# Ten K and V loads of a two-layer decode kernel, cut into two or three transfers by rows

## The chip, the cores and the metric

The kernel runs on one core of a Trainium2 chip. The metric is the device time of one execution in microseconds. Before the change its median is 303.34 us over 2 runs (302.91 and 303.77). A profile is one further execution, taken with the hardware profiler; its own span is named below.

## The reference

One token per batch entry goes through two layers with the same weights. Each layer is attention on a cache, then a gated feed-forward part, both with a residual connection:

```python
B, Sq, D = 4, 1, 512
Hq, Hkv, Sk, Dh = 32, 8, 4096, 128
...
q = (x @ wq) split into 32 heads
k = jnp.repeat(k_cache, rep, axis=1)      # rep = 4 query heads for each K/V head
v = jnp.repeat(v_cache, rep, axis=1)
p = _softmax(q k^T * Dh ** -0.5)
A = (p v, heads side by side) @ wo
...
B = (_sigmoid(x w_gate) * (x w_up)) @ w_down
...
x = x + _A_ref(_layernorm(x), ...)
x = x + _B_ref(_layernorm(x), ...)
x = x + _A_ref(_layernorm(x), ...)
x = x + _B_ref(_layernorm(x), ...)
```

K and V of one batch entry and one K/V head are 4096 x 128 in bf16, 1 MB each. There are 4 x 8 such heads, so 32 MB of K and 32 MB of V, each wanted in both layers.

## The kernel before

**Units.** One pass of attention for one layer, batch entry and K/V head is a unit. `ORDER` (L22) fixes the order of the 64 units, in `seq`; a unit is named by its place there, 0 to 63, so "K 44" is the K cache of unit 44. Units are worked two at a time (a pair): DVE turns each K in 32 x 32 blocks in place (`k_turn`, L1164), PE forms the scores (`scores`, L1180), DVE takes maxima, ACT exponentials (L1265), PE turns them (L1310), ACT or DVE copies them out (L1344, L1338), and PE multiplies them with V (`pv`, L1414). The steps of neighbouring pairs are interleaved, and small matmuls of the projections and the feed-forward part are set between them by tables written out at the head of the file.

**Slots.** A load of K or V takes one of 12 slots in SBUF, each 128 partitions of 8 KB; the four parts of the space of `wq` become four more slots late in the run. Row p of a load is 32 tokens of 128 numbers, so 8 KB that lie together in DRAM go to partition p. Some heads stay in their slots from layer 0 to layer 1 (`RET`, L15) and are not loaded a second time.

**Order of the loads.** The string table `LOADS` (L92) fixes the order of all loads, weights among them; it doesn't depend on what is free. `pump` (L522) is called after most steps: while the next load in the list has a free slot, it hands SyncE one DMA (L550). A slot is free in the list as soon as the code has written the last use of its contents; SyncE itself then waits on the chip until that use has been done (matmul L1414 for V, L1180 for K), and everything behind waits with it, since SyncE issues in order. All loads go through this one queue.

The part of the order that the change touches, units left out that stay in their slots: V 40, **K 44, K 45, V 41, K 46, K 47**, K 48, **V 44, V 45, K 49, V 46, V 47**, V 48, K 52, V 49, K 53, K 54, and so on to V 56, then K 62, K 63 and V 58 to V 63. The loads in bold are the ten that are changed. The last two V loads are issued in four quarters each (`v_parts`, L517), whose pieces are 2 KB.

**Semaphores.** Each slot has a semaphore that its DMAs raise by 16; what uses the slot waits for the value that it has after the slot's latest load. `_Sched` (L194) keeps, for each tile, its last writer and its readers, and derives the waits: `group` (L215) records several instructions of one engine, puts the waits ahead of the first of them and hands the last one's token to later users. `dma` (L244) is `group` with a single function.

```python
            S.dma(
                "sp",
                (lambda dst, src: lambda e: e.dma_start(dst, src))(dst, src),
                f"d{s}" if s < NSLOT else f"wq{s - NSLOT}",
                writes=slot_keys(s),
            )
```

Of the kernel before, what the change touches and what calls it, by code (L numbers as in the profile page):

```python
# [171 lines left out]
)  # L172


class _Token:
# [135 lines left out]
def bass_interleave_layers__gqa_block_cached__glu_gated_glu__decode_kernel(  # L311
# [17 lines left out]
    P = 128  # L329
# [13 lines left out]
    NSLOT = 12  # L343
# [8 lines left out]
    S = _Sched()  # L352
# [144 lines left out]
    def slot_keys(s):  # L497
        return [f"s{s}"] + ([f"wq{s - NSLOT}"] if s >= NSLOT else [])

    def take():  # L500
        return free.pop(0)

    def by_quarters(n):
        return n < NU - 2 and SHARE[n // 2] > 5
# [5 lines left out]
    def v_parts(s, n):  # L510
        _, b, u = seq[n]
        rows = A_v_cache[b, u].rearrange("(a p j) d -> a p (j d)", a=4, p=P)
        for a in range(4):
            dst = slot[s][:, a * JG * DH:(a + 1) * JG * DH]
            S.dma(
                "sp",
                (lambda dst, src: lambda e: e.dma_start(dst, src))(dst, rows[a]),  # L517
                f"wo{4 * (n % 2) + a}",
                writes=[f"v{n % 2}_{a}"] + (slot_keys(s) if a == 0 else []),
            )  # L520

    def pump():  # L522
        while loads:
            kind, n = loads[-1]
            if kind in wparts:
                loads.pop()
                dst, src = wparts[kind](n)
                S.dma("sp", (lambda dst, src: lambda e: e.dma_start(dst, src))(dst, src), f"wo{n}" if kind == "wo" else kind, writes=[f"{kind}{n}"])  # L528
                continue
            if not free:  # L530
                return
            loads.pop()
            s = take()
            _, b, u = seq[n]
            if kind == "k":
                where["kn", n] = s
                src = A_k_cache[b, u].rearrange("(p j) d -> p (j d)", p=P)
            else:
                where["v", b, u] = s
                if n >= NU - 2:  # L540
                    v_parts(s, n)
                    continue
                src = A_v_cache[b, u].rearrange("(p j) d -> p (j d)", p=P)
            dst = slot[s][:, :]
            if kind == "v" and by_quarters(n):
                dst = dst.rearrange("p (a m) -> p a m", a=4)
                src = A_v_cache[b, u].rearrange("(a p j) d -> p a (j d)", a=4, p=P)
            S.dma(
                "sp",
                (lambda dst, src: lambda e: e.dma_start(dst, src))(dst, src),  # L550
                f"d{s}" if s < NSLOT else f"wq{s - NSLOT}",
                writes=slot_keys(s),
            )

# [6 lines left out]
    for k in range(KD):  # L561
        if k == 1:
# [5 lines left out]
            writes=[f"wq{k}"],  # L568
        )
    pump()  # L570

    dve(lambda e: e.memset(ones_f, 1.0), writes=["ones_f"])
# [18 lines left out]
    fns = []  # L591
# [882 lines left out]
    def o_turn(g):  # L1474
        p = g % 2
        many = 2 - PV_WIDE[g]
        s = stage.pop()
        o_raw = slot[s].bitcast(dt.float32)[:, 0:2 * P * many]
        act(lambda e: e.activation(o_raw, O_ps[p][:, 0:2 * P * many], ACTF.Copy), reads=[f"O{p}"], writes=slot_keys(s))
        fns = []  # L1480
        for n in range(2 * many):
            r = n * REP
            fns.append(
                (lambda n, r: lambda e: e.matmul(
                    O_ps[p][:, 0:2 * OW].rearrange("p (t w) -> p t w", t=2)[:, :, 0:REP],
                    lhsT=o_raw[:, n * P:(n + 1) * P],
                    rhs=o_sel[:, :, r:r + REP],
                    start=(n == 0),
                    stop=(n == 2 * many - 1),
                ))(n, r)  # L1490
            )
        S.group("pe", fns, reads=slot_keys(s) + ["o_sel"], writes=[f"O{p}"])
        free.append(s)
        pump()
# [113 lines left out]
    for m in wo_steps.pop((-1, 0), ()):  # L1608
        wo_turn(m, (M_ps, S_ps)[m % 2], "MS"[m % 2])
    k_turn(0)  # L1610
    pump()
    k_turn(1)
    pump()
# [17 lines left out]
    for b in range(Bn):  # L1631
        n = vstep[last[0, b]] - 1
# [499 lines left out]
```

## Time and profile before

| what | value |
|---|---|
| median of 2 runs | 303.34 us |
| span of the profiled execution | 306.1 us |
| PE busy | 224.3 us, 73% |
| DVE busy | 205.7 us, 67% |
| ACT busy | 131.2 us, 43% |
| DMA packets of the kernel's own queue | 93.9% of 16 engines' span |
| bytes read from HBM | 116.66 MB, 381 GB/s over the span |

How to read it: the span runs from the first to the last instruction of the profiled execution; that execution's own time is given by its span alone. The page cuts the span into 40 slices of 7.65 us and gives for each the mean busy share of the 16 DMA engines and what they moved. The chain that ended last is followed back from the last instruction, at each step to whatever released it. A DMA in the chain counts from its issue to its landing, so time in the queue is in it. "SPq" is SyncE, which issues the DMAs; an issue by itself is no busy time of an engine. The windows view gives, for each stretch, the busy time and count of instructions of PE, PE's weight loads, DVE, ACT and POOL, then the granted TensorE clock, the DMA share and the rate. A DMA share can come out a little over 1, since a packet is counted whole where it starts.

### The profile page before, as it was taken

What the parts mean: (1) busy time and instruction counts of PE and PEld (TensorE: products, weight loads), DVE (VectorE), ACT (ScalarE), POOL (GpSimd) and SP (SyncE); (2) the same over time, 40 slices, a digit from 0 to 9 for tenths busy, and PEclk for the clock granted to TensorE, in tenths of its full rate; (3) what the DMA queues carried; (4) which work ended last, traced back from release to release, by engine and by line L of the source; (5) the groups of instructions that cost most, each with busy time, mean ns of one, the idle gap of its engine ahead of it and who ended that gap; (6) DMA issues with size and microseconds to landing.
All of it is one profiled execution on the core that took longest, in us unless ns stands there. A gap on an engine that the chain in (4) does not pass through costs nothing.

```text
span 306.1 us, 11460 instructions
## 1 busy us (share of the span) xinstructions
PE 224.3 (73%) x4993; PEld 157.6 (51%) x4993; DVE 205.7 (67%) x600; ACT 131.2 (43%) x521; POOL 26.0 (9%) x107
## 2 busy tenths in 40 slices
PE   0384386864687888688886777888868688987886
PEld 0331043543464466566554554665546456556676
DVE  4755677885766368875854997566788668357743
ACT  1031243552205246564451874627772443646310
POOL 0000000000000010000001110001000000012200
PEclk9999999999579897979999857589788979599977
DMA  7999999999999979999999999999999999999900
GB/s 283 420 397 415 422 414 416 418 418 421 418 416 403 388 295 418 423 415 416 388 394 378 415 422 421 419 418 422 420 416 418 413 412 415 400 345 411 377 18 3
DMA packets 20094, 117.40 MB, mean 384 GB/s; under 512 B 1992, under 2 KB 1996, under 8 KB 7500
## 3 DMA queue, kind: packets, MB, share of 16 engines
q1 hardware_dynamic: 20044, 116.67, 93.9%
q8 instruction: 39, 0.64, 0.8%
q14 instruction: 11, 0.09, 0.1%
HBM read 116.66 MB, written 0.00 MB: 381 GB/s over the span
## 4 chain that ended last, share of the span: by engine, by line
DMA 45%; PE 30%; DVE 12%; SPq 5%; ACT 4%; issue 3%; POOL 0%; POOLq 0%; DVEq 0%; ACTq 0%
DMA slot<-in_A_v_cache_dram 22%; DMA slot<-in_A_k_cache_dram 12%; PE O_ps L1414 9%; DMA wd<-in_B_w_down_dram 6%; DVE slot L1164 6%; DMA wo<-in_A_wo_dram 5%; PE S_ps L1180 5%; ACT pT L1344 2%; SPq L550 2%; SPq L528 2%; PE M_ps L636 2%; PE O_ps L1566 2%; PE M_ps L1034 1%; PE M_ps L1087 1%; DVE wo L651 1%
## 5 line engine op out<-in xcount | busy, mean ns | idle before, releaser
L1164 DVE STREAM_TRANSPOSE slot<-slot 128x1024 f32<-128x1024 f32 (+1 forms) x61 | 100.9, 1663 | 7.0 <-DMA slot<-in_A_k_cache_dram 6.9
L1344 ACT ACTIVATE pT<-PT 32x64 bf16<-32x64 f32 x392 | 84.3, 215 | 31.9 <-PE PT L1310 26.9
L1414 PE MATMUL O_ps<-pT,slot 128*128 128x32 bf16 (+2 forms) x1888 | 65.8, 190 | 16.2 <-DMA slot<-in_A_v_cache_dram 9.6
L1414 PEld LDWEIGHTS O_ps<-pT,slot 128*128 128x128 bf16 x1888 | 59.6, 101 | 23.3 <-DMA slot<-in_A_v_cache_dram 10.6
L1180 PE MATMUL S_ps<-slot,qz 128*32 128x256 bf16 x1008 | 48.9, 329 | 12.5 <-DVE slot L1164 7.2
L1265 ACT ACTIVATE pe<-S_ps,small 128x256 bf16<-128x256 f32 x32 | 15.2, 474 | 63.3 <-DVE small L1253 63.2
L1180 PEld LDWEIGHTS S_ps<-slot,qz 128*32 128x32 bf16 x1008 | 25.3, 107 | 24.8 <-DVE slot L1164 9.2
L1279 POOL TENSOR_TENSOR small<-small 128x1 f32<-128x1 f32 x64 | 12.4, 193 | 217.6 <-ACT pe L1265 215.1
L646 ACT ACTIVATE wo<-M_ps 128x512 bf16<-128x512 f32 x14 | 8.3, 595 | 35.0 <-PE M_ps L636 35.0
L1338 DVE CAST pT<-PT 32x64 bf16<-32x64 f32 x88 | 19.4, 221 | 5.6 <-PE PT L1310 4.1
L1566 PE MATMUL O_ps<-oT,wo 128*128 128x32 bf16 x576 | 19.7, 188 | 1.1 <-issue 0.5
L636 PE MATMUL M_ps<-wo,row 64*128 64x512 bf16 x56 | 13.3, 565 | 9.1 <-DVE wo L651 5.5
L1566 PEld LDWEIGHTS O_ps<-oT,wo 128*128 128x128 bf16 x576 | 18.2, 101 | 2.1 <-DVE oT L1505 1.1
L1217 DVE TENSOR_REDUCE small<-S_ps 128x1 f32<-128x256 f32 x32 | 13.2, 413 | 8.0 <-PE S_ps L1180 7.8
L903 POOL TENSOR_TENSOR qz<-qc,norm 128x128 bf16<-128x128 bf16 x32 | 12.6, 399 | 45.5 <-ACT qc L889 45.5
L1240 PE MATMUL MS<-row_max,mask_f 128*128 128x16 bf16 x64 | 6.6, 176 | 13.1 <-DVE row_max L1223 12.6
L651 DVE CAST wo<-M_ps 128x512 bf16<-128x512 f32 x14 | 9.5, 680 | 9.6 <-PE M_ps L636 9.5
L1505 DVE TENSOR_TENSOR oT<-O_ps,rden 128x8 bf16<-128x8 f32 x31 | 4.9, 159 | 14.4 <-PE O_ps L1414 9.8
L1240 PEld LDWEIGHTS MS<-row_max,mask_f 128*128 128x128 bf16 x64 | 4.3, 107 | 19.2 <-DVE row_max L1223 17.7
L1199 PE MATMUL MS<-ident_bf 128*128 128x256 bf16 x69 | 12.2, 316 | 0.4
L1310 PE MATMUL PT<-ident_bf,pe 128*128 128x128 bf16 x64 | 10.0, 245 | 2.9 <-ACT pe L1265 2.6
L1253 DVE CUSTOM_DVE_ANT_0 row_max<-MS,small 128x16 bf16<-128x16 f32 x32 | 7.0, 217 | 7.3 <-PE MS L1240 7.1
(143 smaller groups left out, 231.1 us busy)
## 6 DMA issues: line engine op xcount, KB each, us to landing
slot<-in_A_v_cache_dram SPq DMA_DIRECT2D x49, 1024.0 KB, 12.5
slot<-in_A_k_cache_dram SPq DMA_DIRECT2D x43, 1024.0 KB, 11.3
wq<-in_A_wq_dram SPq DMA_DIRECT2D x4, 1024.0 KB, 7.8
wo<-in_A_wo_dram SPq DMA_DIRECT2D x8, 512.0 KB, 15.8
wq<-in_A_v_cache_dram SPq DMA_DIRECT2D x3, 1024.0 KB, 12.3
slot<-in_A_v_cache_dram SPq DMA_DIRECT2D x8, 256.0 KB, 13.6
wg<-in_B_w_gate_dram SPq DMA_DIRECT2D x2, 896.0 KB, 18.9
wu<-in_B_w_up_dram SPq DMA_DIRECT2D x2, 896.0 KB, 16.2
```

What stands on the lines that cost most here:

```text
L636: (lambda h, i, rows: lambda e: e.matmul(ps[h][:, :], lhsT=spread_w[i][rows, :], rhs=wo_sb[rows, c + i, :], start=(i == 0), stop=(i == 1), ...
L651: lambda e: e.tensor_copy(wo_sb[:, c + 1, :], ps[1][:, :]),
L903: lambda e: e.tensor_tensor(qz_sb[z][:, :, 0:4 * REP].rearrange("p i (a r) -> p i a r", r=REP), qc_sb[:, b, u:u + 2, :, :].rearrange("p u ...
L1164: dve(lambda e: e.transpose(kf, kf), writes=[f"s{st}"])
L1180: (lambda t, b2, e_, w0, s: lambda e: e.matmul(S_ps[p][32 * s:32 * s + 8 * REP, 0:2 * P], lhsT=qzf[:, w0:w0 + 8 * REP], rhs=ktv[:, :, s, : ...
L1217: lambda e: e.tensor_reduce(m, S_ps[p][:, 0:2 * P], AX.X, ALU.max),
L1265: lambda e: e.activation(to, frm, ACTF.Exp, bias=nm_sb[p], scale=exp_scale, accum_out=sm_sb[p][0],),
L1279: (lambda n: lambda e: e.tensor_tensor(sm_sb[p][n + 1], sm_sb[p][n], top(sm_sb[p][n]), ALU.subtract))(n),
L1338: (lambda dst, frm: lambda e: e.tensor_copy(dst, frm))(dst, frm),
L1344: (lambda dst, frm: lambda e: e.activation(dst, frm, ACTF.Copy))(dst, frm),
L1414: (lambda x, c, j: lambda e: e.matmul(O_ps[p][:, ul * OW:ul * OW + PV_WIDE[g]].rearrange("p (w n) -> p w n", n=REP), lhsT=vv[:, x * JG + c ...
L1566: (lambda c, r: lambda e: e.matmul(wide_out(O_ps[p], OWO + c, nb), lhsT=wo_sb[:, u * REP + r, bass.ds(2 * P * (c // 2) + c % 2, P, step=2) ...
```

## The change

A table `PARTS` names, for ten loads, the rows of two or three transfers. `pump` makes one `dma_start` for each, all on the slot's own semaphore, each raising it by 16; loads that aren't in the table have one part of 128 rows as before. The waits for the old contents stand ahead of the first part, and later users wait for the value after the last.

```diff
+PARTS = {
+    ("k", 44): (slice(0, 120), slice(120, 128)),
+    ("k", 45): (slice(0, 126), slice(126, 128)),
+    ("v", 41): (slice(0, 104), slice(104, 128)),
+    ("k", 46): (slice(0, 88), slice(88, 128)),
+    ("k", 47): (slice(0, 72), slice(72, 128)),
+    ("v", 44): (slice(0, 120), slice(120, 124), slice(124, 128)),
+    ("v", 45): (slice(0, 63), slice(63, 128)),
+    ("k", 49): (slice(0, 117), slice(117, 123), slice(123, 128)),
+    ("v", 46): (slice(0, 120), slice(120, 125), slice(125, 128)),
+    ("v", 47): (slice(0, 121), slice(121, 128)),
+}
...
-            S.dma(
+            fns = []
+            for rows in PARTS.get((kind, n), (slice(0, P),)):
+                fns.append((lambda dst, src: lambda e: e.dma_start(dst, src))(dst[rows], src[rows]))
+            S.group(
                 "sp",
-                (lambda dst, src: lambda e: e.dma_start(dst, src))(dst, src),
-                f"d{s}" if s < NSLOT else f"wq{s - NSLOT}",
+                fns,
+                sem_key=f"d{s}" if s < NSLOT else f"wq{s - NSLOT}",
+                inc=16,
+                needed=True,
                 writes=slot_keys(s),
             )
```

## The prediction

> **What bounds the kernel now.** I read the page first: the DMA digits and rates, the queue and the chain; then the chain, SyncE's issues and the windows between 200 and 250 us, where the ten loads stand.
>
> ```profile
> span 306.1 us, 11460 instructions
> DMA  7999999999999979999999999999999999999900
> GB/s 283 420 397 415 422 414 416 418 418 421 418 416 403 388 295 418 423 415 416 388 394 378 415 422 421 419 418 422 420 416 418 413 412 415 400 345 411 377 18 3
> q1 hardware_dynamic: 20044, 116.67, 93.9%
> DMA 45%; PE 30%; DVE 12%; SPq 5%; ACT 4%; issue 3%; POOL 0%; POOLq 0%; DVEq 0%; ACTq 0%
> ```
>
> The 16 DMA engines are busy from the start to about 293 us (38 slices of 7.65 us), at 93.9% of 16 engines' span, with a rate that hardly leaves 415 to 422 GB/s. Transfers are the largest share of the chain. So the kernel ends when the last bytes have come, plus a tail of compute.
>
> ```profile
> 207.72 10.57 DMA slot<-in_A_v_cache_dram
> 219.34 13.83 DMA slot<-in_A_k_cache_dram
> 239.34 8.69 DMA slot<-in_A_k_cache_dram
> 248.05 1.85 DVE slot L1164
> ```
>
> These rows of the chain (start, length) are three loads from issue to landing. By the issue order of the code the first is V 41, the second K 49, the third K 53. They land at 218.29, 233.17 and 248.03. From V 41 to K 49 there are six loads, from K 49 to K 53 six more: 14.88/6 = 2.48 and 14.86/6 = 2.48 us a load. A load is 128 rows of 8 KB. The landings come at an even beat, not in bursts, so what counts is a DMA engine's time for its rows: with 128/16 = 8 rows on each, a row costs 2.48/8 = 0.31 us.
>
> ```profile
> 210.00:220.00 10.00, 8.47 (x227) 5.96 (x224) 8.20 (x22) 6.23 (x27) 1.88 (x7) 0.83 1.01 420
> 220.00:230.00 10.00, 6.39 (x155) 4.75 (x152) 7.95 (x16) 7.30 (x32) 0.74 (x3) 0.90 1.01 418
> ```
>
> The last two columns are DMA share and GB/s: no engine has a gap to give away just where the change is made.
>
> How many engines a transfer uses can be read from the small packets. The first row below is the page's; the second is of the window 304 to 306 us, in which only the output is stored.
>
> ```profile
> DMA packets 20094, 117.40 MB, mean 384 GB/s; under 512 B 1992, under 2 KB 1996, under 8 KB 7500
> DMA packets 36, 0.00 MB, mean 2 GB/s; under 512 B 36, under 2 KB 36, under 8 KB 36
> out_dram<-slot SPq DMA_DIRECT2D x1, 4.0 KB
> ```
>
> The store has 4 x 4 x 2 = 32 pieces of 128 B, so four of its 36 packets are something else: a completion mark per engine used. The whole run has 1992 small packets; without the 32 pieces 1960 are left. There are 122 loads with 128 rows, and 122 x 16 = 1952; the other 8 are four each for the two transfers of leading count 4 (the store and the load of x). So a transfer of 128 rows runs on 16 engines, one of 4 on 4: the row count decides it, and an engine gets an equal share.
>
> [...]
>
> **The change part by part.** Each of the ten loads keeps its bytes and slot.
>
> *Rows per engine.* With equal shares of whole rows, the engine count is a divisor of the row count. The largest up to 16: 120 rows on 15, 8 on 8, 126 on 14, 2 on 2, 104 on 13, 24 on 12, 88 on 11, 40 on 10, 72 on 12, 56 on 14, 63 on 9, 65 on 13, 117 on 13, 121 on 11, and 4, 5, 6, 7 and 3 on as many engines. If each transfer starts with the same engine, the first one gets per load 9, 10, 10, 12, 10, 10, 12, 11, 10 and 12 rows: 106 where it had 80. The last gets none. 26 more rows x 0.31 = **+8.06 us** on an engine that had no gap. The others cannot help: a load has landed when its last row has. The bounds: 0 if the starting engine moved on from one transfer to the next so that it evened out; and, since 4 and 128 are both powers of two, a rule of powers of two isn't excluded by the rows: 63, 65, 117, 121 rows would then go through one engine, 469 more rows, 145 us. I take 26, with the divisors that the small packets suggest, and nothing that rotates.
>
> *Thirteen more issues.*
>
> ```profile
> 202.29 4.08 SPq L550 DMA_DIRECT2D slot<-in_A_k_cache_dram  x2
> 207.72 0.33 SPq L550 DMA_DIRECT2D slot<-in_A_v_cache_dram  x1
> 210.74 4.39 SPq L550 DMA_DIRECT2D slot<-in_A_k_cache_dram  x3
> 215.65 2.49 SPq L550 DMA_DIRECT2D slot<-in_A_v_cache_dram  x2
> 219.34 0.33 SPq L550 DMA_DIRECT2D slot<-in_A_k_cache_dram  x1
> 222.70 9.09 SPq L550 DMA_DIRECT2D slot<-in_A_v_cache_dram  x3
> SPq L550 <- PE O_ps L1414: 17.7, 7, 3.4
> SPq L550 <- PE MS L1240: 13.1, 4, 6.6
> ```
>
> An issue takes 0.33 us (rows with x1). Ten loads become 23 transfers, 13 x 0.33 = 4.3 us of SyncE. It waits 17.7 + 13.1 = 30.8 us for its two commonest releasers alone between 200 and 250 us, so this is hidden; and a load of 2.48 us issued 10.57 or 13.83 us before it lands lies 8 us or more in a queue, which covers 0.66 us for a second and third piece. Without cover it would cost at most 0.66 us once. No wait is added: the first piece holds the slot's old wait, all pieces count on the slot's semaphore, and transpose L1164 and matmul L1414 wait for the sum.
>
> *What can absorb a delay.*
>
> ```profile
> 266.00:267.00 1.00, 1.00 (x23) 0.91 (x24) 0.00 (x0) 0.69 (x1) 0.00 (x0) 0.50 0.96 401
> 267.00:268.00 1.00, 0.96 (x9) 0.04 (x8) 0.00 (x0) 0.00 (x0) 0.00 (x0) 0.50 0.57 238
> 268.00:269.00 1.00, 0.97 (x9) 0.12 (x10) 0.00 (x0) 0.00 (x0) 0.00 (x0) 0.50 1.03 303
> ```
>
> Behind the ten loads the engines run dry once, around 267.5: 0.04 + 0.43 = 0.5 us of mean idle. If the most burdened engine has this gap too, it works it off there. If it was among those that finished early, it has up to the whole stretch of three rows, 3 us. I take -0.5; bounds 0 and -3. PE is full there at a granted clock of 0.50, so it gives nothing back.
>
> *The pace of rows in an odd transfer.* Before has no load with rows dealt to 9, 11 or 15 engines. Bounds: the rows keep 0.31 us (0), or two engines get in each other's way in every split load and the 106 rows take twice as long (106 x 0.31 = +32.9). The nearest row is of the other load shape, V in pieces of 2 KB at the end:
>
> ```profile
> 285.00:289.00 4.00, 2.83 (x82) 2.20 (x79) 2.62 (x10) 2.17 (x10) 1.96 (x7) 1.00 1.03 383
> ```
>
> 383 GB/s against 420 at a full share is 9.7% dearer; on 32.9 us that is **+3.2**.
>
> Sum: 8.06 - 0.5 + 3.2 = **+10.8 us**, the span 306.1 + 10.8 = 316.9. The profiled span lies 2.8 us above the median of the runs, 303.34, and I add the difference to that: **314 us**, 3.5% slower. 2%, 6.1 us, is about what a measurement of this kernel tells from no change: 297.3 to 309.4 is "the same".
>
> **The rivals.**
>
> *Rows collide on the way into SBUF.* In an even load, each engine may write rows that no other engine touches at that time; dealt in blocks of 5 to 11 rows the blocks no longer fall on such borders, and two engines that meet share one path. For it: a row's 0.31 us is steady through the span as if something of fixed width set it. Against: no row of before shows two engines meeting. Half of the 106 rows at half pace adds 16.4: 303.3 + 8.06 - 0.5 + 16.4 = 327; all of them 344. [...]
>
> *Not slower: the rows are spread over all 16 anyway.* If the hardware cuts a transfer finer than rows, or the first engine moves on with each transfer, no engine piles up more than a few rows. It decides in the load at 202.29: with two rows or fewer piled up (0.6 us), what is left are 13 hidden issues: 303 to 305. For it: only counts of 4 and 128 are on show. Against: 4 rows did not spread over 16 engines.
>
> *The relieved engines were the late ones.* If the engine that lands last has none of the extra rows and the first engines run ahead by the 3 us of the dry stretch, 8.06 - 3 = +5: 308, still inside 2%.
>
> *Faster.* Only if the relieved engines are what holds each landing and the burdened ones have more slack than 8 us; a share of 1.01 speaks against it.
>
> **How the numbers follow.** Forecast 0.47 (own range 308 to 320); collisions 0.28 (320 to 345); spread over all 16, 0.13; late ones relieved 0.07; faster 0.03 (below 297); powers of two 0.02 (over 400). A low end of 304 leaves out the faster case and half of the spread (303 to 305), 0.10; a high end of 336 leaves out the dear part of the collisions and the last case, about 0.08. So 304 to 336. Faster by over 2%: 0.03. Same: spread 0.13, late ones relieved 0.05, the forecast's low tail 0.03, 0.21. Slower: 0.76.
>
> **What would show it.** Right: between 205 and 240 us GB/s falls by a fifth or so (8 to 11 of some 30 us lost), the three landings slip step by step (V 41 by 1.5 us, K 49 by 6, K 53 by 8 or more), the last 60 us keep their shape. Collisions: the rate halves and the packets' time grows, so that the DMA share stays near 1 while GB/s falls; in my forecast the share falls with the rate, since idle engines cause it. The packets under 512 B decide between the counts: the engine counts above add up to 221 marks instead of 160, so 1992 + 61 = 2053; 23 transfers on 16 engines each would leave 1992 + 208 = 2200. Wrong: GB/s at 415 or more throughout, or SyncE's issues growing well beyond 0.33 us.

## The result, and the profile after

The changed kernel takes 344.69 us (342.45 and 346.94), before 303.34: a ratio of 1.135, interval 1.124 to 1.145. That is 41 us slower, where 11 had been forecast, and outside the stated range of 304 to 336. Three of the kernels below (halves by column, 120/8, and eight rows at a time with only the destination apart) each had one execution in a slower state, at a lower granted clock, which their times leave out.

The page of the changed kernel: the span, the DMA digits and rates in 40 slices (now of 8.63 us), the small packets and the queue.

```profile
span 345.1 us, 11473 instructions
DMA  7999999999995999999999999988889989999940
GB/s 302 415 408 415 417 413 421 420 418 417 407 414 195 416 425 417 415 380 418 408 422 418 419 420 233 202 181 203 183 199 199 220 345 382 372 336 360 408 160 4
DMA packets 20155, 117.40 MB, mean 340 GB/s; under 512 B 2053, under 2 KB 2057, under 8 KB 7561
q1 hardware_dynamic: 20105, 116.67, 92.1%
```

Up to slice 24 the rate is the old one but for a dip in slice 13, which before has in slice 15. Then it halves for eight slices, about 69 us (207 to 276 us), while the engines' busy digit stays at 8 and 9. So the engines are mostly not waiting for work: each row takes longer. The 2053 small packets are 1992 - 160 + 221: exactly the 221 completion marks that the engine counts of the prediction add up to.

The chain of the changed kernel has the last piece of V 41, the last piece of K 49, and K 53:

```profile
206.53 24.40 DMA slot<-in_A_v_cache_dram
232.74 33.03 DMA slot<-in_A_k_cache_dram
274.05 13.15 DMA slot<-in_A_k_cache_dram
```

They land at 230.93, 265.77 and 287.20, later than before by 12.6, 32.6 and 39.2 us. The span is longer by 39.0. All of it is lost between 206 and 287 us, and nothing is won back or lost behind K 53.

The windows of the slow stretch in the changed kernel (its last columns are granted clock, DMA share and GB/s; before had 1.01 and 420 there):

```profile
210.00:270.00 60.00, 22.16 (x480) 16.08 (x480) 21.27 (x50) 14.80 (x65) 3.35 (x13) 0.60 0.89 196
```

From share and rate comes the mean price of an 8 KB row, by which the kernels below are compared. It is the busy time that an engine spends for each 8 KB, taken over all loads in the window, whole ones as well. Sixteen engines busy for a share s of the time move GB/s = s x 16 x 8.192 KB / price, so price = 131 x s / (GB/s) us. Before: 131 x 1.01 / 420 = 0.315 (0.31 by the landings). Changed: 131 x 0.89 / 196 = **0.595**. The share of 0.89 means that a ninth of the engines' time is idle as well.

The waits of the changed kernel (total in us, times, longest) say who pays:

```profile
DVE slot L1183 <- DMA slot<-in_A_k_cache_dram: 34.4, 10, 9.8
PE O_ps L1433 <- DMA slot<-in_A_v_cache_dram: 28.3, 13, 7.6
```

In the rows of before these were 6.9 and 9.6 us; the transposes and the products with V stand and wait for rows.

### The profile page after: what moved, and what is told of

Same layout as the page of the kernel before. It is cut to its first block, busy times and chain, and to the rows that moved or that the text cites. A ratio compares the mean times of both kernels' runs of the same rounds, so it can differ in the third digit from the quotient of the medians.

```text
span 345.1 us, 11473 instructions
## 1 busy us (share of the span) xinstructions
PE 229.4 (66%) x4993; PEld 159.7 (46%) x4993; DVE 206.1 (60%) x600; ACT 130.9 (38%) x521; POOL 26.0 (8%) x107
## 2 busy tenths in 40 slices
DMA packets 20155, 117.40 MB, mean 340 GB/s; under 512 B 2053, under 2 KB 2057, under 8 KB 7561
## 4 chain that ended last, share of the span: by engine, by line
DMA 45%; PE 27%; DVE 15%; SPq 4%; issue 4%; ACT 3%; POOL 0%; POOLq 0%; DVEq 0%; ACTq 0%
DMA slot<-in_A_k_cache_dram 18%; DMA slot<-in_A_v_cache_dram 18%; DVE slot L1183 9%; PE O_ps L1433 7%; DMA wd<-in_B_w_down_dram 5%; PE S_ps L1199 5%; DMA wo<-in_A_wo_dram 4%; PE M_ps L1053 2%; SPq L564 2%; SPq L542 2%; DVE small L1236 1%; PE O_ps L1585 1%; PE M_ps L655 1%; ACT pT L1363 1%; DVE pT L1357 1%
## 5 line engine op out<-in xcount | busy, mean ns | idle before, releaser
L1183 DVE STREAM_TRANSPOSE slot<-slot 128x1024 f32<-128x1024 f32 (+1 forms) x61 | 101.2, 1664 | 34.6 <-DMA slot<-in_A_k_cache_dram 34.4
L1433 PE MATMUL O_ps<-pT,slot 128*128 128x32 bf16 (+2 forms) x1888 | 67.0, 192 | 37.4 <-DMA slot<-in_A_v_cache_dram 28.3
L1433 PEld LDWEIGHTS O_ps<-pT,slot 128*128 128x128 bf16 x1888 | 61.1, 102 | 44.3 <-DMA slot<-in_A_v_cache_dram 25.7
L1199 PE MATMUL S_ps<-slot,qz 128*32 128x256 bf16 x1008 | 50.7, 338 | 23.6 <-DVE slot L1183 15.3
L922 POOL TENSOR_TENSOR qz<-qc,norm 128x128 bf16<-128x128 bf16 x32 | 12.6, 399 | 44.8 <-ACT qc L908 44.8
L1218 PE MATMUL MS<-ident_bf 128*128 128x256 bf16 x69 | 12.9, 328 | 0.4
```

The lines of the kernel that those rows point to most:

```text
L922: lambda e: e.tensor_tensor(qz_sb[z][:, :, 0:4 * REP].rearrange("p i (a r) -> p i a r", r=REP), qc_sb[:, b, u:u + 2, :, :].rearrange("p u ...
L1183: dve(lambda e: e.transpose(kf, kf), writes=[f"s{st}"])
L1199: (lambda t, b2, e_, w0, s: lambda e: e.matmul(S_ps[p][32 * s:32 * s + 8 * REP, 0:2 * P], lhsT=qzf[:, w0:w0 + 8 * REP], rhs=ktv[:, :, s, : ...
L1218: lambda e: e.matmul(MS[:, 2 * P:4 * P].rearrange("p (i m) -> p i m", i=2), lhsT=ident_bf[:, :], rhs=wide_id, start=True, stop=True,)
L1433: (lambda x, c, j: lambda e: e.matmul(O_ps[p][:, ul * OW:ul * OW + PV_WIDE[g]].rearrange("p (w n) -> p w n", n=REP), lhsT=vv[:, x * JG + c ...
```

## The experiments

Three theories were on the table. **Theory 1**: rows of different engines meet on the way into SBUF and halve each other's pace. **Theory 2**: rows pile up on the first engines, the forecast's main term. **Theory 3**: cutting loads, the additional issues, or row counts that 16 doesn't divide have a price by themselves. All kernels below keep the change's loop and replace `PARTS` (where the table gives a pair, the loop takes the destination's and the source's slice from it, or rows and columns); `TEN` is the list of the ten loads.

### More transfers alone: halves by column

```diff
+PARTS = {t: ((slice(0, 128), slice(0, 2048)), (slice(0, 128), slice(2048, 4096))) for t in TEN}
```

> Each of the ten loads is two transfers of all 128 rows, the first half of each row and then the second half (4 KB pieces): more issues (20 instead of 10), but 16 engines, equal shares and the old rows for each engine. Theory 1 (engines whose rows lie in the same part of SBUF halve each other's pace): no collisions beyond those of before, so within 1 us of before, 303 to 305. Theory 2 (rows pile up on the first engines): no pile, 303 to 305. Theory 3 (cutting a load and its additional issues cost the time): like the changed kernel in part, 10 us or more slower, 313 to 345.

304.09 us against 304.35, ratio 1.000, interval 0.996 to 1.004. Ten more issues and twice as many pieces cost nothing that can be measured. Theory 3 loses its first half.

### Divisible by 16, no pile: 64/64 and 112/16

```diff
+PARTS = {t: (slice(0, 64), slice(64, 128)) for t in TEN}
...
+PARTS = {t: (slice(0, 112), slice(112, 128)) for t in TEN}
```

> Each of the ten loads is two transfers of 64 rows (0 to 63, 64 to 127): divisible by 16, four rows to each of 16 engines in each, nothing piles up. Theory 1 (collisions in SBUF; by the profile of the changed kernel a row took about twice 0.31 us there): two engines meet on each part of SBUF, ten loads of 2.48 us take up to twice as long, 20 to 35 us slower, 323 to 338, with the DMA share near 1 at half the rate. Theory 2 (pile of rows on the first engines): no pile, 303 to 306. Theory 3 (row counts that 16 does not divide): 303 to 306.

> Each of the ten loads is a transfer of 112 rows (seven for each of 16 engines) and one of 16 (one each): equal shares, no pile, both counts divisible by 16, but an engine's rows no longer lie where those of a 128-row load lie. Theory 1 (collisions): 20 to 40 us slower, 323 to 343. Theory 2 (pile): 303 to 306. Theory 3 (row counts that 16 does not divide): 303 to 306.

329.12 us (ratio 1.083, 1.073 to 1.093) and 328.29 us (1.080, 1.071 to 1.089), against 304.35: 25 and 24 us slower. Here all 16 engines have equal shares (2152 small packets in both, 1992 - 160 + 320: 16 marks for each of the 20 transfers) and nothing piles up. The windows of the slow stretch, 64/64 first, then 112/16:

```profile
210.00:250.00 40.00, 19.07 (x393) 13.69 (x385) 16.01 (x35) 13.27 (x59) 2.27 (x10) 0.59 1.02 237
```

```profile
210.00:255.00 45.00, 19.70 (x409) 14.15 (x409) 18.97 (x40) 13.72 (x61) 2.78 (x11) 0.58 1.02 233
```

The share is full, the rate 237 and 233: prices of 0.564 and 0.574 us. The engines are all at work and a row costs nearly twice as much. Neither the pile nor the divisor explains this: Theory 2 and the second half of Theory 3 expected 303 to 306.

### The same rows, engines and bytes in another place

Half of each load alone, the same source rows, to partitions 0 to 63 or to 32 to 95:

```diff
+PARTS = {t: ((slice(0, 64), slice(0, 64)),) for t in TEN}     # (destination, source)
...
+PARTS = {t: ((slice(32, 96), slice(0, 64)),) for t in TEN}
```

> Half of the ten loads is left out: each is one transfer that brings rows 0 to 63 of the source to partitions 0 to 63, and the other 64 rows aren't loaded. 16 engines, four rows each, no pile. [...] From the rows: the 64/64 kernel needed about 2 x 2.48 us for a load in two such halves, so a half costs 2.48, as much as a whole load of before, and the time stays near 303, with packets of 0.55 us. Without collisions: 10 x 1.24 = 12 us less, 291 (or a little more, where compute becomes the bound).

> As the kernel with partitions 0 to 63, half of the ten loads left out, the same source rows, the same engines and rows per engine; only the destination differs: partitions 32 to 95. [...] Any theory in which the number of rows, of engines or of transfers sets the pace: the same time for both.

313.12 us for 0 to 63 (311.22 and 315.02; ratio 1.031, 1.016 to 1.046), 299.37 us for 32 to 95 (298.55 and 300.19; 0.985, 0.979 to 0.992), both against 303.92 of before. Against before neither is clear of 2%, but the two are clear of each other: only the destination's first partition differs, and 13.8 us lie between them. So where the rows land in SBUF sets their pace; rows, number of engines (16 for 64 rows, by the marks of 64/64), transfers and source are the same in both. The windows from 210 us, first 0 to 63, then 32 to 95:

```profile
210.00:235.00 25.00, 16.41 (x378) 12.38 (x371) 15.91 (x34) 12.64 (x55) 3.30 (x13) 0.66 1.01 213
```

```profile
210.00:230.00 20.00, 15.97 (x442) 12.42 (x435) 17.49 (x42) 13.34 (x58) 3.34 (x13) 0.91 0.82 283
```

With 0 to 63 the engines are full at 213 GB/s, 0.62 us a row: half the bytes take longer than the whole loads did. With 32 to 95 they idle for 18% of the stretch and still move a third more. Two sizes were off. 0 to 63 was expected at 303: a row has the expected price, 0.62, so that a half load costs the 2.48 us of a whole one, yet the kernel came out 9 us higher. Loads that were left whole pay too, as a wider window of the kernel with 0 to 63 shows:

```profile
206.00:240.00 34.00, 22.82 (x532) 16.54 (x528) 22.42 (x57) 16.84 (x72) 3.35 (x13) 0.73 1.01 212
```

In these 34 us the engines moved 34 x 212 = 7.2 MB at 0.62 us a row, and the ten half loads hold only 5.2 MB; the other 2 MB belong to whole loads. 32 to 95 came out above the 291 that ten half loads without collisions had been put at: with a share of 0.82 the DMA engines no longer set the pace (in the chain from 195 to 260 us DMA has 12%). The formula gives 131 x 0.82 / 283 = 0.38 us a row there, well below 0.62 but not down to 0.315; the view doesn't tell why.

What in the place makes the difference no view shows. Taking in partitions 32 to 95 is not enough, though: the 112 rows of 112/16 include them, and a row cost 0.574 us there. The author's reading is that it hangs on which rows are under way at the same time. That these meet is argued from the prices; no view shows a single row.

### The transfer to 32 to 95 between two others

```diff
+PARTS = {t: (slice(0, 32), slice(32, 96), slice(96, 128)) for t in TEN}
```

> Each of the ten loads is three transfers: rows 0 to 31, 32 to 95, 96 to 127; all counts divisible by 16, two, four and two rows for each engine, nothing left out, no pile. [...] If any transfer of fewer than 128 rows is slow by itself: 328 or more. If the pile alone counts: 303 to 306.

331.61 us, ratio 1.089 (1.078 to 1.100): 27 us slower. The price of a row in the stretch is 131 x 1.02 / 229 = 0.584:

```profile
210.00:255.00 45.00, 18.42 (x411) 13.57 (x395) 17.88 (x35) 14.28 (x63) 3.37 (x13) 0.65 1.02 229
```

Had the middle half kept the price of before and only the outer half paid as in 64/64 (25 us for all rows), it would have cost half of that, about 12 us, by estimate. So my way of pricing, each transfer by its own place, is wrong. The middle half didn't stay cheap. The time falls where "any transfer of fewer than 128 rows is slow by itself" was expected, 328 or more; against that rival stands the kernel with 32 to 95, whose 64 rows were not slow (0.38 us). A possible reason is that the engines aren't in step, so that the middle rows of one meet the outer rows of another. That whole loads paid beside those to 0 to 63 fits this, but no run tests it, and it stays an argument.

### The pile alone

To 32 to 95, where a row cost 0.38 us, go 64 rows of each load, and four loads bring 17 more rows in a second transfer, to partitions 0 to 16; 17 is prime. The other rows are left out.

```diff
+PARTS = {t: ((slice(32, 96), slice(0, 64)),) for t in TEN}
+for t in (("v", 41), ("k", 47), ("v", 45), ("v", 46)):
+    PARTS[t] += ((slice(0, 17), slice(64, 81)),)
```

> The ten loads bring only 64 rows, to partitions 32 to 95 (299.4 us in the kernel that has nothing else), and four of them (V 41, K 47, V 45, V 46) in a second transfer 17 more rows, to partitions 0 to 16; the other 47 or 64 rows are left out. 17 is prime, so all 17 rows run on one engine. If that is always the engine that begins the others too, it carries 40 + 68 = 108 rows, as many as the first engine in the change (106; 80 before), without meeting another engine. Pile theory, the first term of the forecast: 28 rows above before, 303.6 + 8.7 - 0.5 = 312, and packets of 0.31 us; at least 306. If rows on few engines cost nothing, because the starting engine moves on or the queue covers it: 299 to 302.

313.72 us against 304.10, ratio 1.030 (1.022 to 1.039); 312 was expected, and 299.37 without the 17 rows. The page and the windows:

```profile
DMA packets 19526, 112.71 MB, mean 360 GB/s; under 512 B 1996, under 2 KB 2000, under 8 KB 7504
```

```profile
220.00:250.00 30.00, 16.64 (x385) 12.98 (x386) 14.41 (x37) 9.63 (x42) 2.22 (x9) 0.78 0.52 173
```

1996 small packets are 1992 + 4: one mark for each of the four transfers, so 17 rows do run on a single engine. The share falls to 0.52: nearly half of the engines' time is idle. That is what a pile looks like, and it's quite unlike the changed kernel's 0.89 at half rate. The pile is real: the 17 rows cost 14 us, and the time is within 2 us of what the forecast's term gives. That is in part luck, for the formula gives 131 x 0.52 / 173 = 0.39 us a row here, not 0.31, and whether the 17 rows met others isn't shown. That it's always the same engine isn't shown by this run alone either; the time fits 108 rows on one.

### What the other 17 us are

64/64 and 112/16 cost 24 to 25, the change 41. Three more kernels vary the pile, with all ten loads cut alike (120/8: 90 rows on the first engines; 88/40: 120 rows, if both transfers of a load begin with the same engine, which no view shows), or with the change's cuts rounded to multiples of 16 (80 rows):

```diff
+PARTS = {t: (slice(0, 120), slice(120, 128)) for t in TEN}
...
+    ("k", 44): (slice(0, 112), slice(112, 128)),     # k45, v44, k49, v46, v47 alike
+    ("v", 41): (slice(0, 96), slice(96, 128)),
+    ("k", 46): (slice(0, 80), slice(80, 128)),       # k47 alike
+    ("v", 45): (slice(0, 64), slice(64, 128)),
...
+PARTS = {t: (slice(0, 88), slice(88, 128)) for t in TEN}
```

> All ten loads as 120 and 8 rows (15 engines with eight rows each, then eight engines with one). Pile: 10 rows, +3.1 us. [...] If the pile hides behind the collisions: 325 to 329. If not being divisible by 16 has a price of its own (fewer engines, uneven shares): 335 or more, near the change itself (345).

> The ten cuts of the change, each in two transfers with counts rounded to multiples of 16: 112/16 six times, 96/32, 80/48 twice, 64/64. 16 engines with equal shares, no pile. If the pile at the dear row price is what the change costs beyond 24 us: 80 rows at about 0.6 us, 48 us instead of 24.8, +23, 324 to 332. If it is the cuts themselves, wherever they lie: 338 or more.

> All ten loads as 88 and 40 rows (11 engines with eight rows, then ten with four): 120 rows on each of the first ten engines, a pile of 40. If pile and collisions multiply, as 106 rows at 0.6 us do for the change (63.6 - 24.8 = +39): 120 rows at 0.5 to 0.6 us are 60 to 72, +35 to +47, 339 to 351. If they add, with the pile at 0.31: 24 + 12.4 = +36, 338 to 342. If the pile hides behind the collisions, as with 120/8: 325 to 332.

The small packets are 2062 for 120/8, 2042 for 88/40 and 2152 for the rounded cuts: less the 1832 of all the rest, 23, 21 and 32 marks for each of the ten loads, as 15 + 8, 11 + 10 and 16 + 16 engines give.

Measured: 324.72 us for 120/8 (one execution, before 304.10), 331.14 for the rounded cuts (ratio 1.083, 1.070 to 1.096), 337.79 for 88/40 (1.104, 1.087 to 1.121). Rounding takes away the pile and leaves the cuts (and three third pieces, where ten more transfers cost nothing above), and 15 of the 41 us go. 120/8 costs no more than 112/16, 21 us against 24, so row counts that 16 doesn't divide show no price of their own; it came out at the low edge of "the pile hides behind the collisions". 88/40 came out a little under both branches in which the pile counts (338 or more), and clear of the one in which it hides (332 at most). The windows, in the order 120/8, rounded, 88/40:

```profile
210.00:250.00 40.00, 19.73 (x423) 14.36 (x422) 18.75 (x39) 14.25 (x64) 3.35 (x13) 0.64 0.98 263
```

```profile
210.00:255.00 45.00, 19.41 (x385) 14.15 (x377) 18.02 (x35) 13.02 (x57) 2.21 (x9) 0.54 1.02 223
```

```profile
210.00:260.00 50.00, 19.72 (x419) 14.21 (x415) 18.21 (x41) 14.85 (x65) 3.36 (x13) 0.59 0.80 211
```

Rows of the fullest engine (with the same first engine for every transfer) times the price of a row in the same run, less the 80 x 0.315 = 25.2 us of before:

| kernel | rows of the fullest engine | price, us | product less 25.2 | measured |
|---|---|---|---|---|
| 64/64 | 80 | 0.564 | +19.9 | +24.8 |
| 112/16 | 80 | 0.574 | +20.7 | +23.9 |
| rounded cuts | 80 | 0.600 | +22.8 | +26.0 |
| 120/8 | 90 | 0.488 | +18.7 | +20.6 |
| 88/40 | 120 | 0.497 | +34.4 | +32.6 |
| the change | 106 | 0.595 | +37.9 | +41.4 |

The product gives nearly the order, and the size within 5 us, mostly too low. It is an account, not a forecast, since the price is taken from each run itself; and that the price is lower with 120/8 and 88/40 (0.49) than with equal shares (0.56 to 0.60) nobody foresaw. Fewer engines at a time meeting less often would fit those two, but the change has uneven shares as well and paid 0.595; why the two are cheaper stays open.

### Eight rows at a time

Three loads (K 45, V 44, V 46) in 16 transfers of eight rows, each on eight engines (2328 small packets with the rows apart: 1992 - 48 + 48 x 8; that they are the same eight each time no view shows), with rows four apart or side by side in source and destination:

```diff
+NEAR = [slice(8 * i, 8 * i + 8) for i in range(16)]
+APART = [slice(32 * (i // 4) + i % 4, 32 * (i // 4) + i % 4 + 29, 4) for i in range(16)]
+PARTS = {t: tuple(zip(APART, APART)) for t in THREE}      # rows apart on both sides
...
+PARTS = {t: tuple(zip(NEAR, NEAR)) for t in THREE}        # side by side on both sides
...
+PARTS = {t: tuple(zip(APART, NEAR)) for t in THREE}       # destination apart, source side by side
```

> Three loads (K 45, V 44, V 46) are 16 transfers of 8 rows each, with the rows four partitions apart (r, r+4, ... r+28). All 48 transfers run on the same eight engines, which get 16 rows of each of the three loads where they had 8: 24 more rows, a pile as high as that of the change (26), while rows that move at the same time lie in different parts of SBUF. Pile theory, and the first term of the forecast: 24 x 0.31 = +7.4 us, 309 to 312; SyncE needs 16 x 0.33 = 5.3 us for the issues of a load, which may add 1 to 3. If piles cost nothing, 303 to 305; if every transfer with fewer than 16 engines is slow for another reason than where its rows lie, 320 or more.

> The same three loads in 16 transfers of 8 rows as the kernel with rows four apart, the same eight engines and the same pile of 24 rows, but with eight neighbouring rows in each transfer. [...] Pile and issues alone: no slower than 317.

> The three loads in 16 transfers of 8 rows: neighbouring rows of the source go to partitions four apart, so that rows of these loads land in other partitions than the reference wants (the computation is changed by that). Tells whether the pace hangs on the source or on the destination, and whether the 0.62 us that an issue took with rows four apart came from the source. Theory 1 (destination): packets at 0.31 us, time as with rows four apart or, if the issues are cheaper, only the pile: 309 to 317. [...]

Apart: 317.09 us (ratio 1.044, 1.033 to 1.054). Side by side: 326.39 (1.074, 1.061 to 1.088). Destination apart, source side by side: 314.74 (one execution). The first is 5 us above its expectation, and SyncE's issues show why. Each row below is a run of 17 issues (start, length), the 16 pieces of V 44 and one more load, in the order of the three kernels:

```profile
215.19 11.13 SPq L557 DMA_DIRECT2D slot<-in_A_v_cache_dram  x17
213.00 5.78 SPq L557 DMA_DIRECT2D slot<-in_A_v_cache_dram  x17
214.79 11.17 SPq L557 DMA_DIRECT2D slot<-in_A_v_cache_dram  x17
```

With the destination's rows four apart an issue takes about 11.13/17 = 0.65 us with the gap behind it (0.62 without it in the chain), side by side 0.34. So the 16 issues of a load need 10 us and the DMA engines run short (in 210 to 215 us their share is 0.45):

```profile
210.00:215.00 5.00, 2.98 (x85) 2.19 (x85) 2.72 (x4) 2.90 (x14) 0.38 (x2) 1.00 0.45 139
```

So the number for "rows apart" isn't a clean price of a pile; it was the reason for the kernel with 17 rows. What remains is the comparison. These are the windows of the whole stretch, apart first, then side by side:

```profile
210.00:250.00 40.00, 21.68 (x512) 17.14 (x513) 21.09 (x51) 14.48 (x63) 3.33 (x14) 0.79 0.85 311
```

```profile
210.00:250.00 40.00, 20.69 (x454) 15.08 (x454) 20.09 (x45) 14.31 (x64) 3.37 (x13) 0.64 0.91 274
```

The kernel with the cheaper issues is 9 us slower, and its rows are dearer, 0.435 us against 0.358, which fits neighbouring rows that meet. Changing the order of the source alone made nothing slower (317.09 and 314.74), changing that of the destination alone did (314.74 and 326.39). Pile and issues alone had been expected to bring side by side to no more than 317.

## Why the prediction was wrong, point by point

**Right.** *The bound*: the loads' beat sets the end; what was lost up to K 53 (39.2 us) is what the span lost (39.0). *The engine counts*: 2053 small packets, to the packet. The list took the largest divisor up to 16 for each row count; 1996 with the 17 rows, 2062 with 120/8 and 2042 with 88/40 agree with it too. *The issues*: ten more cost nothing with halves by column. *The pile*: with 28 more rows on one engine 313.7 us was measured and 312 expected, though a row cost 0.39 us there. That every transfer begins with the same engine, from which the 26 rows follow, no view shows; the time with the 17 rows fits it. *The form of the sum*: see below. *What can absorb*: little, 0.2 us where 0.5 was taken. *The shape of the last 60 us*: 58.1 us from K 53's landing to the end before, 57.9 after. Two readings were rough: 38 slices of 7.65 us end at 290.7 us, not at about 293, and only 22 of the 38 lie within 415 to 422 GB/s; neither bears on the sum.

**Wrong: the pace of rows in an odd transfer.** This term was put at +3.2 us between bounds of 0 and +32.9, by the nearest row of the trace, the V quarters with 2 KB pieces. That row was near in the list and far in kind: its pieces are shorter, but its loads cover all 128 partitions, like every K and V load of before. With the prices of the runs the term is 106 x (0.595 - 0.315) = **+29.7 us**, close to the upper bound. No row of before bears on it, so the two ends were all the trace could give, and nothing in it spoke for a value near the lower one. The form of the sum held: the term prices all 106 rows, the pile among them, and 8.06 - 0.5 + 29.7 = +37.3 against the 41.4 measured. The 4 us between them stay open.

**Wrong with it: the chance of the collision rival.** Its mechanism fits the runs, and its sign came: half the rate at a share that stays high (0.89, with a ninth idle as the forecast's pile would have it). It was given 0.28, and the range was cut at 336, below its dear end, "all of them 344". That this number met the 344.69 measured is partly luck: it stands for twice the price, 0.62, and the changed kernel paid 0.595, with 4 us more that no term explains.

**The other rivals.** Rows spread over all 16 engines: excluded by 2053 instead of 2200 packets. Powers of two: excluded by the same number. Late engines relieved, and faster: nothing of it is seen.

## What to carry to other kernels

By these runs a transfer of 128 rows isn't only 16 equal shares: its rows also land where they don't hold each other up (0.315 us a row). Fewer rows can come near that (32 to 95 alone, 0.38) or lose it (0 to 63 at 0.62, 112/16 at 0.574, 32/64/32 at 0.584), and divisibility by 16 didn't tell which. When a kernel is bound by loads, look at rate and DMA share together. Here a full share at about half the rate (1.02 and 237 GB/s with 64/64) went with dear rows, and a falling share with engines that had nothing to do, because of a pile (0.52) or because the loads no longer set the pace (0.82). To cut a load, cut its columns: halves by column cost nothing here.

## What the runs showed of the hardware that was not expected

- Five ways to load by rows with equal shares came out at nearly the same price: 0.56 to 0.62 us a row for 64/64, 112/16, 32/64/32, the rounded cuts and 0 to 63 alone.
- A transfer to 32 to 95, at 0.38 us a row when alone, gains nothing between two others: 32/64/32 cost 27 us, 64/64 25.
- With the uneven shares of 120/8 and 88/40 a row was cheaper, 0.488 and 0.497 us, but not with those of the change, 0.595. Why is open.
- Whole loads slow down beside loads to partitions 0 to 63: 7.2 MB went at 0.62 us a row, and the half loads are 5.2 MB of it.
- An issue with the destination's rows four partitions apart takes SyncE 0.62 us instead of 0.33; with the source's rows side by side it takes as long (11.17 us for 17 issues, against 11.13).
